# A new issue order and engine choice for all pieces of an attention and mixing kernel

## The chip, the cores and the metric

The kernel runs on one core of a Trainium2 chip. That core has five engines with a queue of their own each: TensorE (PE, with its weight loads shown as PEld), VectorE (DVE), ScalarE (ACT), GpSimd (POOL) and SyncE (SP), which here only issues DMAs. An engine takes its instructions strictly in the order in which the program issues them to it; engines wait for each other through semaphores. The metric is the device time of one execution in microseconds (us). Inputs are drawn at random with a fixed seed and come as 64-bit floats.

## The reference, cut to what matters

```python
# q, k, v: (8, 8, 576, 64); w_theta, w_ch: (512, 512); w_tok_r, w_tok_i: (576, 576)
k_p = k.reshape(B, H, 72, 8, D).mean(axis=3)
v_p = v.reshape(B, H, 72, 8, D).mean(axis=3)
scores = scale * np.matmul(q, k_p.transpose(0, 1, 3, 2))
scores = scores - np.max(scores, axis=-1, keepdims=True)
attn = np.exp(scores)
attn = attn / (np.sum(attn, axis=-1, keepdims=True) + 1e-09)
x = np.matmul(attn, v_p)            # heads joined: (8, 576, 512)
theta = x @ w_theta
zr, zi = x * np.cos(theta), x * np.sin(theta)
y = einsum('ts,bsd->btd', w_tok_r, zr) + einsum('ts,bsd->btd', w_tok_i, zi)
u = x + y
out = u + np.maximum(u @ w_ch, 0.0)
```

## The kernel before, in words

The work is cut into streams, one Python generator for each small unit, and each `yield` in a generator ends a piece. A stream's name is a letter, a batch b (0 to 7) and a number. A written list, SCHEDULE (line 30), names streams word by word: each word issues the next piece of its stream. A last letter v, g or a on a word gives the engine of a piece that has a choice: VectorE, GpSimd or ScalarE. Since an engine takes its instructions in order, the list fixes the order of every queue, SP's DMA queue among them. Waits on data and on buffers are put in by the framework; a buffer with one copy makes its next writer wait for the last reader.

The streams, with the pieces that matter here:

- k, v (`load`) and Q (`queries`): DMAs of batch b; Q then has one VectorE transpose. K b.j and V b.j (`pool`) add up groups of eight rows (line 408, 413) on VectorE or GpSimd; V of batch 0 does so on TensorE (`pool_on_pe`). K b (`keys`) turns the pooled keys into kpT; V b (`vals`) lays out the pooled values (lines 537 to 556).
- h, c (`channel_weights`) and w (`token_weights`): DMA a slice of the 64-bit weights, make 32-bit values of it with five VectorE pieces and one ScalarE piece (`to_f32`, lines 280 to 299), and split h and c into a high and a low part (lines 178, 331). W (`turn_weights`) transposes the token weights on TensorE (line 382) and splits them into WTh and WTl (line 373).
- S b.m (`soften`): scores of 128 rows (TensorE, line 583), maximum, exponential, sum, reciprocal, and the multiply en by the reciprocal (line 644, small remainder line 653), then a transpose. E b (`turn`): sixteen DMAs per group (line 728) finish that transpose, then copies and subtractions give eh, er, ev (lines 742, 749).
- X b.g.c (`attend`): the product with the values (line 775) and its copy to xT.
- T b.m (`rotate`), eleven pieces: xh (a copy, line 176 or 178), xl (a subtraction, line 791), the product pt with w_theta (line 798, twelve matmuls), g on ScalarE (line 802), g on VectorE (line 804), four transposes into the PSUM bank px (line 808), sine, absolute value, cosine (lines 815 to 823), and two products z with px on VectorE (lines 825, 827). px has one bank, pt has one bank (th).
- Z b.c (`take`): zh (copy) and zl (subtraction, line 849). M b.c.hf (`mix`): the token product py (line 862, 27 matmuls), the sum u (line 868), uh (copy), ul (subtraction, line 875). F b.c.hf (`final`): the channel product pf (line 890, 12 matmuls), oT (line 896), the transpose R (line 909, R has one buffer) and four DMAs out (line 915).

A copy shows as line 176 when ScalarE does it and as line 178 on VectorE or GpSimd. Products with high and low parts are sums of three products, which is why each value comes as a pair.

The loop that carries out the list (line 991) is

```python
for word in SCHEDULE.split():
    name, engine = (word[:-1], word[-1]) if word[-1] in "vga" else (word, None)
    now[0] = engine
    next(streams[name])
```

Of the kernel before, what the change touches and what calls it, by code (L numbers as in the profile page):

```python
# [35 lines left out]
S0.2 w0.1v w2.1 w1.1 h3 S0.2g k1.1 w1.1 S0.0a S0.1a S0.4 S0.1 w1.0 S0.2g S0.3 S0.2 S0.1v h3 S0.4 S0.3 w2.0
w1.0 S0.4 X0.0.0 w1.0 S0.3g S0.3v w2.0 h3 w1.0 w2.0 S0.3 h3 w1.0 X0.0.0a S0.4 W0 S0.2a S0.4 Q1.0 w1.0 S0.3a
w1.1 w4.0 h3 X0.0.1 w1.0g W0v Q1.1 h3v S0.2 K1.1g X0.0.1a S0.2v w2.1 S0.4v X0.0.2 S0.4v h3v S0.3 S0.4
X0.0.2a S0.3a S0.4v X0.0.3 W0 w2.0 v1.0 S0.4 K1 X0.0.3a w1.1v K1.2g T0.0a W0 T0.1a w2.0 S0.4v X0.2.0 w3.0
w2.1 T0.0g Q1.1 v1.2 W0a K1a T0.0 X0.2.0a T0.1g w2.1 c0 V1.0v w2.1 K1 X0.2.1 w3.0 T0.0 v1.1 w2.0 w2.1 K1a  # L40
T0.0 X0.2.2 w2.1 X0.2.1v w3.0 T0.0 T0.0 w2.0g W0 w2.1v X0.2.3 X0.2.2a T0.0a w4.0 w3.0 T0.1 T0.0 T0.0 w4.0
V1.1g w3.0 w3.1 T0.0 X0.2.3a w3.0 T0.2a w3.1 W1 T0.1 T0.3v w3.1 T0.2g c0 T0.2 T0.1 W1a V1v w3.1 V1v W1 V1.2g
T0.1 T0.1 T0.1a T0.1 c0 W1 w3.1 T0.2 X0.2.3g k2.2 W1v w4.0 V1 W1 T0.2 T0.2 w4.0 W2 T0.4a T0.1 T0.2 w3.1 T0.1
W2a w4.0 T0.3g T0.3 w3.1v T0.2a W2 T0.2 w3.0g T0.2 W2 T0.3 w4.0 T0.2 W2a T0.3 T0.3 T0.4g T0.4 c0 T0.3 W2 V1v
T0.3a w4.0g V1v T0.3 T0.3 W3 T0.4 c0 T0.3 T0.4 T0.4 W3a c0 T0.4 c0 W3 T0.4 c1 T0.4 W3 c0v W3a Z0.0a W3 c0v
W4 c0v Z0.1a Z0.0v M0.0.0 c1 W4v Z0.1v W4 M0.1.0 c1 W4a M0.0.0 W4 M0.0.0a c1 W4v M0.0.0v W4 c1 W4v c1 W4 c1
M0.0.1 M0.1.0 M0.1.0a c2 c1g M0.1.0v c1v c1g M0.1.1 Z0.2v M0.0.1 c2 Z0.2g M0.0.1a c2 M0.0.1v c2 S1.0 Z0.3a
M0.1.1 M0.1.1v c2 M0.2.0 S1.0 Z0.3g M0.1.1v S1.0 c2 c2 c3 c2v M0.3.0 M0.2.0 c2a M0.2.0v S1.0 M0.2.0v S1.0v
S1.0g c2v c3 S1.1 M0.3.0 c3 M0.3.0a S1.0 S1.1 M0.3.0g M0.2.1 S1.0a c3 S1.1 S1.0 c3 c3 c3 S1.0 S1.1 S1.2
S1.0a M0.2.1 Q2.0 S1.1g S1.1v c3v M0.2.1a M0.3.1 S1.2 S1.0 S1.2 c3v c3g M0.2.1v S1.1 k2.0 M0.3.1 F0.0.0  # L50
S1.1a S1.2 M0.3.1a S1.1 S1.1 M0.3.1v S1.3 S1.2g S1.1v F0.0.1 S1.3 S1.2g K2.0g S1.1 S1.3 F0.0.0 S1.2 F0.0.1
X1.0.0 F0.0.0 F0.1.0 X1.0.0v F0.0.1 F0.0.1 X1.0.1 S1.3 S1.4 F0.1.0 X1.0.1v k2.1 X1.0.2 S1.4 F0.1.1 X1.0.2v
Q2.0 X1.0.3 F0.2.0 S1.2a F0.1.0 Q2.1 X1.0.3a F0.1.1 S1.2 T1.0a S1.2 F0.2.1 S1.2a F0.2.0 S1.3g T1.0v T1.1a
S1.2 S1.3g T1.0 T1.1v S1.4 F0.1.1 K2.1v K2.2g F0.1.1 F0.2.1 S1.3 Q2.1 T1.0 v2.2 F0.3.0 S1.3a v2.0 S1.3 S1.3
F0.3.1 S1.4 S1.3a Q3.0 F0.2.0 S1.4g S1.4v F0.3.0 T1.0 T1.0 S1.3 S1.4 T1.0 F0.2.1 T1.1 V2.0g S1.4v T1.0a
F0.2.1 F0.3.1 S1.4 T1.0 T1.0 T1.0 S1.4 K2 T1.1 S1.4v v2.1 K2a S1.4 T1.1 T1.1 X1.2.0 T1.1 K2 X1.2.0v K2a
T1.1a F0.3.0 X1.2.1 F0.3.1 T1.1 S2.0 T1.1 F0.3.1 X1.2.1a T1.1 V2.1g X1.2.2 S2.0 X1.2.2a X1.2.3 X1.2.3a S2.1
S2.0 V2.2g k3.0 T1.2v V2v T1.2v T1.2 V2v k3.2 T1.3a S2.0 V2 T1.3g X1.2.3v T1.2 T1.4v S2.0g T1.2 T1.2 T1.2
S2.0g S2.1 T1.3 K3.0g T1.2a S2.0 T1.2 T1.2 S2.1 S2.2 T1.2 V2g k3.1 T1.4g V2v T1.3 S2.1 T1.3 T1.3 S2.1g S2.1v
T1.3 S2.2 T1.4 K3.1g T1.3a T1.3 S2.1 S2.2 T1.3 E2.0 T1.3 K3.2g S2.2 S2.3 T1.4 T1.4 S2.2g T1.4 T1.4 K3 T1.4  # L60
S2.2g S2.3 T1.4 S2.3 S2.4 Z1.0v Z1.1a K3v Z1.0v M1.0.0 Z1.1v v3.2 Q3.0 M1.0.1 v3.0 M1.0.0 E2.0a Q3.1 E2.0v
E2.0g S2.2 M1.0.0a S2.3 E2.0g M1.1.0 Z1.2a M1.0.1 S2.3v M1.0.1a S2.3v S2.3 V3.0g S2.4 X2.0.0 M1.1.1 X2.0.0a
Q3.1 S2.4 Z1.2g v3.1 S2.4 Q4.0 M1.1.0 M1.0.0v X2.0.1 M1.1.0v S2.4g Z1.3a M1.0.1v K3 M1.2.0 X2.0.1v K3v
M1.1.0v V3.1g Z1.3v M1.1.1 V3.2v M1.1.1a X2.0.2 k4.0 M1.2.0 S3.0 X2.0.2a M1.1.1v M1.2.0v S2.4v X2.0.3 S2.4
k4.2 M1.2.1 X2.0.3v E2.2 M1.2.0v S3.0 T2.0v S3.0 T2.1v T2.0g K4.0v M1.3.0 T2.1g S3.0 M1.2.1 S3.0g M1.2.1a
S3.1 M1.3.0 S3.0g M1.3.0v M1.2.1g M1.3.1 S3.1 M1.3.0g S3.1 S3.1 k4.1 S3.2 M1.3.1 M1.3.1a F1.0.0 M1.3.1g S3.0
E2.2a E2.2v T2.0 E2.2g E2.2v S3.1g F1.0.0 S3.1v X2.2.0 S3.2 T2.0 K4.1g F1.0.1 X2.2.0a T2.0 S3.2 X2.2.1
F1.0.1 T2.0 T2.0 S3.2 T2.1 v4.0 F1.0.1 F1.0.0 X2.2.1a K4.2v T2.0a F1.0.1 T2.0 T2.0 X2.2.2 T2.0 S3.3 X2.2.2a
v4.2 S3.1 T2.1 X2.2.3 T2.1 S3.2g T2.1 E3.0 X2.2.3a F1.1.0 V3v X2.2.3a T2.1 S3.2g T2.2v T2.3v T2.2g T2.1a
S3.3 T2.2 T2.1 T2.3g T2.1 S3.3 T2.1 F1.1.0 F1.1.1 T2.2 T2.4v F1.1.0 T2.2 T2.2 T2.4v T2.2 T2.3 S3.3 T2.2a  # L70
F1.1.1 T2.2 T2.2 T2.2 F1.2.0 F1.1.1 T2.3 V3v V4.0g V3 F1.1.1 T2.3 T2.3 S3.4 F1.2.0 V3g T2.3 V3g T2.3v T2.4
v4.1 E3.0a Q4.0 T2.3 T2.3 E3.0a Q4.1 E3.0g T2.3 F1.2.1 F1.2.0 T2.4 S3.2 E3.0g T2.4 T2.4 F1.3.0 F1.2.1 T2.4
F1.2.1 T2.4 F1.2.1 F1.3.1 S3.3g T2.4 F1.3.0 Z2.0a S3.3g S3.4 V4.1g X3.0.0 K4 Z2.1a Z2.0v M2.0.0 S3.4 Z2.1g
k5.0 K4v F1.3.1 Q4.1 M2.0.1 M2.0.0 Q5.0 X3.0.0v M2.0.0a V4.2v K5.0v k5.2 M2.1.0 Z2.2a M2.0.1 k5.1 M2.0.0v
F1.3.1 M2.0.1a Z2.2g S3.3 S3.4 K4 M2.0.1v X3.0.1 K4v M2.1.1 M2.1.0 X3.0.1v M2.1.0v K5.1g S3.4v S3.4v F1.3.0
S3.4 F1.3.1 X3.0.2 M2.1.0g M2.1.1 Z2.3a S4.0 X3.0.2v v5.0 K5.2g M2.1.1v X3.0.3 S4.0 M2.2.0 E3.2 Z2.3g
X3.0.3v S4.0 T3.0a T3.1v S4.0 T3.0g M2.2.1 M2.2.0 M2.2.0a M2.2.0v M2.1.1g S4.0g T3.1g M2.3.0 M2.2.1 M2.2.1v
S4.0g M2.2.1g S4.1 M2.3.0 v5.2 M2.3.0v M2.3.1 M2.3.0g S4.1 E3.2v E3.2a S4.1 E3.2v E3.2g S4.0 F2.0.0 M2.3.1
S4.1 S4.2 M2.3.1v S4.1g S4.1v X3.2.0 F2.0.0 S4.2 T3.0 X3.2.0a M2.3.1g S4.1 S4.2 F2.0.0 X3.2.1 S4.2 T3.0
F2.0.1 X3.2.1a T3.0 S4.2g X3.2.2 F2.0.1 S4.2g T3.0 T3.0 F2.0.1 S4.3 X3.2.2v F2.0.1 T3.0v T3.0 T3.0 X3.2.3  # L80
S4.3 T3.1 X3.2.3a E4.0 V4a X3.2.3g T3.2v S4.3 T3.0 T3.2g V4v S4.4 T3.1 T3.3v V5.0g S4.3 V4 F2.1.0 T3.1 T3.1
Q5.0 T3.1 T3.2 T3.3g T3.1a F2.1.0 F2.1.0 T3.1 V4g T3.1 V4g T3.1 F2.1.1 T3.4v T3.2 T3.4g T3.2 T3.2 F2.2.0
F2.1.1 T3.2 v5.1 F2.1.1 T3.2a T3.3 T3.2 T3.2 F2.2.0 Q5.1 S4.2 E4.0a T3.2 S4.3g E4.0a F2.1.1 S4.3v S4.4
F2.2.1 V5.1g T3.3 T3.3 S4.4 T3.3 F2.3.0 S4.3 E4.0g F2.2.1 k6.0 T3.3 S4.4 T3.4 E4.0g Q5.1 T3.3a T3.3 F2.2.0
Q6.0 T3.3 F2.3.1 V5.2g T3.3 F2.2.1 T3.4 F2.3.0 X4.0.0 F2.2.1 F2.3.1 K5 K6.0g T3.4 X4.0.0a T3.4 K5a X4.0.1
# [944 lines left out]
```

## Time and profile before

| | us |
|---|---|
| median of 3 runs (677.22 to 685.16) | 682.79 |
| profiled execution, device time | 678.47 |
| its span, first to last instruction | 676.6 |
| TensorE matmul busy in it | 599.3 |
| VectorE busy | 569.1 |
| ScalarE busy | 315.7 |
| GpSimd busy | 288.4 |

The mean granted TensorE clock was 0.955 of full speed. A busy time is the union of the engine's instructions; groups give the sum or mean of single instructions, which overlap a little at their ends. "Idle before, releaser" is the time in which the engine waited ahead of an instruction of the group, and whose instruction ended the wait. In the rows, `L862 PE MATMUL py<-WTh,zh` reads: line 862, TensorE, output py from WTh and zh.

### The profile page before, as it was taken

What the parts mean: (1) busy time and instruction counts of PE and PEld (TensorE: products, weight loads), DVE (VectorE), ACT (ScalarE), POOL (GpSimd) and SP (SyncE); (2) the same over time, 40 slices, a digit from 0 to 9 for tenths busy, and PEclk for the clock granted to TensorE, in tenths of its full rate; (3) what the DMA queues carried; (4) which work ended last, traced back from release to release, by engine and by line L of the source; (5) the groups of instructions that cost most, each with busy time, mean ns of one, the idle gap of its engine ahead of it and who ended that gap; (6) DMA issues with size and microseconds to landing.
All of it is one profiled execution on the core that took longest, in us unless ns stands there. A gap on an engine that the chain in (4) does not pass through costs nothing.

```text
span 676.6 us, 11101 instructions
## 1 busy us (share of the span) xinstructions
PE 599.3 (89%) x3891; PEld 547.4 (81%) x3891; DVE 569.1 (84%) x1068; ACT 315.7 (47%) x640; POOL 288.4 (43%) x300
## 2 busy tenths in 40 slices
PE   0758967899769899989799999999999999999996
...
DVE  4899998899899999897999999999986788546634
...
PEclk9865977999988999999999999999999999999999
DMA  9998201236725535655275404582443132402204
...
DMA packets 243992, 57.83 MB, mean 85 GB/s; under 512 B 232032, under 2 KB 232544, under 8 KB 243936
## 3 DMA queue, kind: packets, MB, share of 16 engines
...
q14 instruction: 25, 0.20, 0.1%
...
## 4 chain that ended last, share of the span: by engine, by line
DVE 37%; PE 36%; SPq 9%; DMA 6%; issue 5%; ACT 4%; POOL 2%; DVEq 0%; ACTq 0%; POOLq 0%
PE py L862 14%; PE pt L798 8%; PE pf L890 8%; SPq L728 5%; PE pv L775 3%; DVE mx L613 2%; PE s L583 2%; DMA eraw<-G 2%; DVE g L804 2%; DVE kpst L408 2%; SPq L499 2%; DVE sm L634 2%; DVE en L653 1%; DVE G L665 1%; DVE ul L875 1%
## 5 line engine op out<-in xcount | busy, mean ns | idle before, releaser
L862 PE MATMUL py<-WTh,zh 128*128 128x288 f32 x576 | 87.8, 300 | 2.3 <-DVE xT L868 2.0
L862 PE MATMUL py<-WTl,zh 128*128 128x288 f32 x576 | 87.2, 296 | 0.0
L862 PE MATMUL py<-WTh,zl 128*128 128x288 f32 x576 | 85.6, 298 | 0.9 <-DVE xT L868 0.9
L862 PEld LDWEIGHTS py<-WTh,zh 128*128 128x128 f32 x576 | 80.6, 191 | 4.1 <-DVE xT L868 2.4
L862 PEld LDWEIGHTS py<-WTh,zl 128*128 128x128 f32 x576 | 79.6, 190 | 1.2 <-DVE xT L868 1.1
L862 PEld LDWEIGHTS py<-WTl,zh 128*128 128x128 f32 x576 | 80.6, 189 | 0.0
L644 POOL TENSOR_TENSOR en<-e,ri 128x512 f32<-128x512 f32 (+1 forms) x30 | 33.2, 1108 | 70.2 <-DVE ri L641 40.3
L791 POOL TENSOR_TENSOR xl<-xT,xh 128x512 fp32r<-128x512 f32 x27 | 40.6, 1510 | 50.2 <-DVE xh L178 31.4
L798 PE MATMUL pt<-th,xh 128*128 128x512 f32 x160 | 47.8, 421 | 10.1 <-DVE g L804 10.0
L176 ACT CAST uh<-xT 128x288 fp32r<-128x288 f32 x37 | 15.9, 432 | 81.2 <-DVE xT L868 81.1
L583 PE MATMUL s<-kpT,qT 128*128 128x144 f32 (+1 forms) x320 | 48.5, 298 | 5.5 <-DVE e L628 3.5
L849 POOL TENSOR_TENSOR zl<-z,zh 128x1152 fp32r<-128x1152 f32 x12 | 32.2, 2689 | 43.7 <-ACT zh L176 42.1
L868 DVE TENSOR_TENSOR xT<-py,xT 128x288 f32<-128x288 f32 x64 | 28.0, 439 | 27.1 <-PE py L862 27.0
L583 PEld LDWEIGHTS s<-kpT,qT 128*128 128x128 f32 (+1 forms) x320 | 42.9, 185 | 8.5 <-issue 5.2
L890 PE MATMUL pf<-uh,chh 128*128 128x288 f32 x256 | 46.0, 301 | 0.4 <-DVE oT L896 0.4
L798 PE MATMUL pt<-th,xl 128*128 128x512 f32 x160 | 44.2, 399 | 0.4 <-DVE xl L791 0.4
L890 PE MATMUL pf<-ul,chh 128*128 128x288 f32 x256 | 44.3, 295 | 0.0
L890 PE MATMUL pf<-uh,chl 128*128 128x288 f32 x256 | 44.2, 294 | 0.0
L798 PE MATMUL pt<-tl,xh 128*128 128x512 f32 x160 | 44.2, 399 | 0.0
L802 ACT ACTIVATE g<-pt,c_magic 128x512 f32<-128x512 f32 x38 | 26.1, 686 | 38.4 <-PE pt L798 23.8
L798 PEld LDWEIGHTS pt<-th,xh 128*128 128x128 f32 x160 | 28.4, 195 | 18.0 <-DVE g L804 11.4
L890 PEld LDWEIGHTS pf<-uh,chh 128*128 128x128 f32 x256 | 38.1, 189 | 2.6 <-DVE oT L896 1.0
...
## 6 DMA issues: line engine op xcount, KB each, us to landing
...
```

The costliest lines, as they stand in the source:

```text
L176: nc.scalar.copy(out, src)
L583: nc.tensor.matmul(scs[c // 2][:n, 2 * SP * (c % 2) : 2 * SP * (c % 2 + 1)], qT[:, c, t0 : t0 + n], kpT[:, c, :], start=True, stop=True,)
L644: ENG[pick()].tensor_tensor(en[:n, 0:512].rearrange("p (h g) -> p h g", h=8), e[:n, :, 0:GM], ri[:n].unsqueeze(2).broadcast_to([n, 8, GM]) ...
L728: nc.sync.dma_start(blocks(Ex, jj, i), blocks(Gx, i, jj))
L775: nc.tensor.matmul(pv[:, :gn], l, r, start=i == 0, stop=i == len(terms) - 1)
L791: ENG[pick()].tensor_tensor(xl, xT[:, :, o], f32(xh), ALU.subtract)
L798: nc.tensor.matmul(pt, l[:, c, :], r[:, c, :], start=i == 0, stop=i == 11)
L802: nc.scalar.activation(g, pt, AF.Identity, bias=c_magic)
L849: ENG[pick()].tensor_tensor(zl, z[:, :, o], f32(zh), ALU.subtract)
L862: nc.tensor.matmul(py[:, :HALF], l[:, kk, :], r[:, kk, t], start=i == 0, stop=i == 3 * NK - 1)
L868: nc.vector.tensor_tensor(u, py[:, :HALF], u, ALU.add)
L890: nc.tensor.matmul(pv[:, :HALF], l[:, kk, o], uhl[r][:, kk, t], start=i == 0, stop=i == 11)
```

## The change: what it does

The list is written anew: the same 1882 words by stream and count, in another order, and 309 of the 661 words with an engine letter have another letter. Two small edits in the code let pieces of one stream family come in any order: the buffer of pooled rows is made by whichever piece comes first, not by piece 0 or 1 (no instruction is added by it). The pieces themselves stay.

How often each engine has a piece, before and after, for the kinds that change most:

| piece | ACT | DVE | POOL |
|---|---|---|---|
| uh copy of M (64) | 37, 32 | 27, 11 | 0, 21 |
| ul subtraction of M (64) | | 40, 28 | 24, 36 |
| xh copy of T (40) | 17, 19 | 23, 9 | 0, 12 |
| xl subtraction of T (40) | | 13, 14 | 27, 26 |
| zh copy of Z (32) | 25, 22 | 7, 2 | 0, 8 |
| zl subtraction of Z (32) | | 20, 18 | 12, 14 |
| multiply en of S (40) | | 8, 21 | 32, 19 |
| copy to xT of X (64) | 40, 46 | 24, 18 | |
| eh copy of E (12) | 10, 5 | 2, 3 | 0, 4 |
| er subtraction of E (12) | | 2, 4 | 10, 8 |
| ev subtraction of E (12) | | 4, 7 | 8, 5 |
| pooling of K, batch 1 on (14 large) | | 6, 2 | 8, 12 |
| pooling of V, batch 1 on (14 large) | | 1, 5 | 13, 9 |

Order, in the places that the prediction speaks of. The loads begin with w0.0 k0.1 Q0.0 k0.0 k0.2 h0 v0.0 Q0.1 before, and with k0.0 k0.2 k0.1 w0.0 h0 h2 Q0.0 Q0.1 after; w4.0 is issued ahead of v1.0 before, and behind v1.1 after. On VectorE V1's first piece and W1's split stood in the order V1, W1 before; after, V1's first piece is ScalarE's and comes later. Of the ten c0 pieces, all are ahead of the first py before and five after. In batch 7 TensorE's queue reads, with pt and px for the two TensorE pieces of a rotation: pt 7.2, F6.1.0, px 7.2, pt 7.3, F6.1.1, px 7.3 before, and pt 7.2, px 7.2, F6.1.1, pt 7.3, px 7.3 after.

The diff, cut to the first and the last lines of the list and the code:

```diff
 SCHEDULE = """
-w0.0 k0.1 Q0.0 k0.0 w0.0 w0.0 k0.2 w0.0 h0 w0.0 v0.0 w0.0 w0.0 Q0.1 w0.0g Q0.0 K0.0v h2 K0.1v K0.2g h1 K0.0g
-K0.1g h0 K0.0v v0.1 K0.2g h0 K0.1g K0.2v h0 K0 h0 v0.2 V0.0 K0a h3 h0 h0 w0.1 h0 Q0.1 w1.1 K0 K0a S0.0 h0v
...
-T7.1 T7.1 F6.0.1 T7.2 T7.1a T7.3v F6.0.1 T7.1 X7.2.3g T7.1 F6.0.1 T7.1 F6.1.0 T7.4v T7.2 T7.4g T7.2 T7.2
-F6.1.0 T7.2 T7.3 F6.1.0 T7.2a T7.2 T7.2 T7.2 F6.1.1 T7.3 T7.3 T7.3 F6.1.1 T7.3 T7.4 F6.1.1 T7.3a F6.1.1 T7.3
...
+k0.0 K0.0v K0.0g k0.2 K0.2g k0.1 K0.1v K0.1v K0.1g w0.0 w0.0 w0.0 w0.0 K0.0g K0 w0.0 w0.0 h0 h2 h0 h2 h0 h0 h2
+h2 h0 h0 h2 w0.0 K0a K0.2v K0.2g K0 K0a Q0.0 Q0.0 h0 h0 h0a h0g h2 w0.0v Q0.1 Q0.1 S0.0 h1 h1 h2 S0.0 S0.0 S0.0
...
+T7.1 X7.2.3 X7.2.3a T7.3v T7.2a M6.3.1g M6.2.1g F6.0.1 F6.0.1 F6.0.1 T7.1 T7.1a T7.1 T7.1 T7.2g T7.1 T7.2 T7.2
+F6.0.1 T7.2 T7.2 T7.2 T7.2a T7.2 F6.1.1 F6.1.1 T7.2 T7.2 T7.3g T7.3 T7.3 T7.3 T7.3 T7.3 T7.3a T7.3 F6.1.0 F6.1.0
...
+M7.1.0 M7.0.0v M7.1.0 M7.0.1 M7.0.1 M7.0.1v M7.0.1v M7.1.0g M7.1.0g Z7.2g M7.1.1 Z7.2g M7.1.1 M7.2.0 M7.1.1g
+M7.2.0 M7.2.1 M7.2.1 M7.0.0g M7.2.0a M7.2.1a M7.2.1v Z7.3g Z7.3g M7.3.0 M7.3.0 M7.3.0a M7.2.0v M7.3.1 M7.3.1
...
@@ -442,9 +439,9 @@
...
+        if (name, b) not in pooled:
+            pooled[name, b] = [work([P, NC, D], F32, name, f"{name}{b}"), None]
         if j < 2:
-            if (name, b) not in pooled:
-                pooled[name, b] = [work([P, NC, D], F32, name, f"{name}{b}"), None]
             dst = pooled[name, b][0][:, 2 * j : 2 * j + 2, :]
...
     def pool_on_pe(b, name, j, st):
         steps = [dict(start=r == 0, stop=r == POOL - 1) for r in range(POOL)]
-        if j == 0:
+        if (name, b) not in pooled:
             pv = bank([P, 512], "th", f"pvp{b}")
```

More of the change, by code (lines that the diff above doesn't have):

```diff
@@ L36 @@
[L36 to L85, printed above, removed]
```

143 lines of the change are left out of this document (94 added, 49 removed).

## Prediction

> **What bounds the kernel now.** I read the page first (busy shares and the 40 slices), then the table of five stages, then what TensorE waited for, then the groups of instructions that change their engine. The page:
> ```profile
> PE 599.3 (89%) x3891; PEld 547.4 (81%) x3891; DVE 569.1 (84%) x1068; ACT 315.7 (47%) x640; POOL 288.4 (43%) x300
> ...
> PE   0758967899769899989799999999999999999996
> ...
> DVE  4899998899899999897999999999986788546634
> ...
> PEclk9865977999988999999999999999999999999999
> DMA  9998201236725535655275404582443132402204
> ```
> PE is at 9 nearly throughout the second half, and there the order of the other engines can win little. In slices 3 to 19 both PE and DVE are at 7 to 9, and neither alone is the bound. So I cut the span where the stages change: the first scores (23 us), the first mixing product M0.0.0 (108), that of batch 1 (205), that of batch 7 (630). Each row has the length, then busy us and count of PE, PEld, DVE, ACT and POOL, the granted clock and the DMA share:
> ```profile
> 0.00:23.00 23.00, 5.20 (x22) 4.00 (x22) 12.01 (x24) 4.88 (x9) 8.16 (x15) 1.00 0.98 202
> 23.00:108.00 85.00, 60.74 (x256) 42.81 (x257) 82.60 (x159) 49.18 (x150) 40.78 (x35) 0.74 0.55 130
> 108.00:205.00 97.00, 84.47 (x539) 77.00 (x538) 86.23 (x174) 55.84 (x158) 42.32 (x53) 0.94 0.39 81
> 205.00:630.00 425.00, 407.74 (x2770) 382.65 (x2769) 366.23 (x676) 202.19 (x319) 193.68 (x195) 1.00 0.42 77
> 630.00:677.00 47.00, 41.14 (x311) 40.90 (x309) 22.04 (x39) 3.65 (x7) 3.48 (x2) 0.97 0.20 35
> ```
> Up to 23 us the DMA engines set the pace (share 0.98). From 23 to 108 it is VectorE, with 82.6 of 85 us busy, while PE idles 24.3 us. From 108 to 205 PE idles 12.5 us and DVE 10.8: they take turns. From 205 on PE idles 17.3 of 425 us, and that is all that any order can win there. What PE waited for, in total us, times, and the longest:
> ```profile
> PE wt L382 <- DVE WTl L373: 10.3, 2, 5.9
> PE pt L798 <- DVE g L804: 10.0, 9, 3.5
> PE pe L677 <- POOL spare L644: 4.0, 1, 4.0
> PE s L583 <- DVE e L628: 3.5, 2, 3.0
> ```
> DVE releases most of it. The first and third row lie wholly in the stage from 23 to 108.
>
> **The change part by part.** The instructions stay: no shape, DMA or product changes. What moves is place in each queue and, for part of the copies and subtractions, the engine. The groups that change most (busy us, mean ns), then the copies with min/median/max ns:
> ```profile
> L791 POOL TENSOR_TENSOR xl<-xT,xh 128x512 fp32r<-128x512 f32 x27 | 40.6, 1510 | 50.2 <-DVE xh L178 31.4 <-ACT xh L176 18.0 <-PE pf L890 0.6
> L644 POOL TENSOR_TENSOR en<-e,ri 128x512 f32<-128x512 f32 (+1 forms) x30 | 33.2, 1108 | 70.2 <-DVE ri L641 40.3 <-DVE G L668 16.0 <-ACT g L802 7.0
> L849 POOL TENSOR_TENSOR zl<-z,zh 128x1152 fp32r<-128x1152 f32 x12 | 32.2, 2689 | 43.7 <-ACT zh L176 42.1 <-DVE zh L178 1.6
> L875 DVE TENSOR_TENSOR ul<-xT,uh 128x288 fp32r<-128x288 f32 x40 | 27.6, 690 | 5.5 <-ACT uh L176 5.1
> L875 POOL TENSOR_TENSOR ul<-xT,uh 128x288 fp32r<-128x288 f32 x24 | 19.5, 814 | 46.5 <-ACT uh L176 39.4 <-DVE uh L178 7.0
> L178 DVE CAST xh<-xT 128x512 fp32r<-128x512 f32 x23 | 16.7, 740 | 1.0 <-ACT xT L176 0.8
> L178 DVE CAST uh<-xT 128x288 fp32r<-128x288 f32 x27 | 14.4, 532 | 0.5
> L644 DVE TENSOR_TENSOR en<-e,ri 128x512 f32<-128x512 f32 (+1 forms) x8 | 6.4, 804 | 0.0
> ```
> ```profile
> L178 DVE CAST uh<-xT x27: 258/310/2523, 125.7 to 648.9; 128x288 fp32r<-128x288 f32 x27
> L178 DVE CAST xh<-xT x23: 377/420/3873, 81.3 to 612.2; 128x512 fp32r<-128x512 f32 x23
> L178 DVE CAST zh<-z x7: 1295/1341/1353, 120.2 to 637.0; 128x1152 fp32r<-128x1152 f32 x7
> L178 POOL COPY xT<-xT x5: 387/398/860, 83.0 to 610.1; 128x256 f32<-128x256 f32 x5
> ```
> The counts are those of the table of the change. DVE loses 16 uh x 0.53 = 8.5 us, 12 ul x 0.69 = 8.3, 14 xh x 0.74 = 10.4 and 5 zh x 1.34 = 6.7, and gains 13 multiplies by the reciprocal x 0.80 = 10.4: 23.5 us less of 569. The other moves go both ways, and I take them as nothing. POOL gains 12 ul x 0.81 = 9.8 us and casts that it has not done before: 21 uh, 12 xh, 8 zh. Its nearest row is the copy of 256 elements in 398 ns, 1.55 ns an element, which gives 0.45, 0.79 and 1.79 us, or 33.2 us in all; the two-input row (2689 ns for 1152, 2.33 an element) bounds them above at 50. I take the copy's price, since a cast also reads one input. POOL loses 13 multiplies x 1.11 = 14.4. Net about +29 us, at most +45, on 288. ACT gains some 7 us on 316 and stays far from full.
>
> VectorE and GpSimd slow each other. Both cast rows have a mean far above the median: 27 x (0.532 - 0.310) = 6.0 us and 23 x (0.740 - 0.420) = 7.4 us were lost, with single casts of 2.5 and 3.9 us. So taking 30 of those 50 casts off DVE removes victims as well, and more POOL work hits those left.
> [...]
>
> *Start to 108 us.* Loads: k of batch 0 is now issued first, h2 moves ahead of the queries and v0.0 behind them; ahead of the first scores stand the same number of bytes (v0.0 and h2 are half a megabyte each), so these start near 23 us again. DVE has h2's steps to do meanwhile. Ahead of M0.0.0, 15 steps come to DVE (four xl, three multiplies, one pooling of K1, small ones) and 25 leave its queue (five of c0, four of V1, theta and W casts to ACT); at some 0.8 us for what comes and 0.7 for what goes that is 12 against 17.5, 5 us less. POOL is relieved too: 4 xl x 1.51 and the long multiply below alone are 10.5 us. The rows show that multiply on POOL, a copy of V1 on DVE, and PE's wait that ends with the split of W1:
> ```profile
> 37.36 4.46 POOL L644 TENSOR_TENSOR spare<-spare,ri 128x512 f32<-128x512 f32 x1 [4.49 <-DVE ri L641]
> ...
> 83.39 3.06 DVE L178 CAST Vh<-vp 64x256 fp32r<-64x256 f32 x2
> ...
> 89.32 0.47 PE L382 MATMUL wt<-ident,wsrc_a 128*128 128x128 f32 x1 [5.89 <-DVE WTl L373]
> ```
> The multiply takes 4.46 us on POOL (0.80 on DVE), and PE's 4.0 us wait is for it. Vh stands ahead of WTl on DVE; in the new order V1's first step goes to ACT and W1's WTl follows its copy with nothing of V1 between. I take another 3 us for this: **-8 us** for the stage. Best case the two waits of 14.3 us, worst +3 if w4.0, now issued behind v1.0 and v1.1, comes late.
>
> *108 to 205 us.* The c steps put off above come here, V1's steps go to POOL and ACT, and DVE comes out about even. PE and DVE alternate as before: **-2 us**, between -6 and +4.
>
> *205 to 630 us.* DVE is at 366 of 425 us and gets most of its relief of 23 us here. PE's 17.3 us of idle time go mostly to DVE releases; I take a third of it, **-5 us**, because the rotations get tighter covers (first rival). Bounds -12 and +9.
>
> *Tail.* Same order of products, the last out transfers as before: 0. The new POOL chain of batch 7 (zh and zl of chunks 1 to 3, 4.5 us each at the prices above) fits under the two products py of each chunk, whose row stands with the first rival.
>
> Sum -15 us. The profiled execution took 678.5 us (span 676.6, with 1.9 around it), the median of the runs 682.8, 4.3 more. 678.5 - 15 = 663.5; I add 1.5 for a part of that offset and say **665 us**.
>
> **The rivals.** *Slower: the transposes px wait for the rotation before them.* px has one bank. The transposes of rotation m+1 can start only when the second product with px of rotation m is done. One such chain, with the cover now:
> ```profile
> 611.32 1.08 PE L798 MATMUL pt<-th,xl 128*128 128x512 f32 x4
> ...
> 612.44 0.69 ACT L802 ACTIVATE g<-pt,c_magic 128x512 f32<-128x512 f32 x1 [1.71 <-PE pt L798]
> ...
> 613.16 0.69 DVE L804 SCALAR_TENSOR_TENSOR g<-g,pt 128x512 f32<-128x512 f32 x1 [0.57 <-ACT g L802]
> ...
> 615.21 0.72 ACT L823 ACTIVATE g<-g,c_cos 128x512 f32<-128x512 f32 x1
> ...
> 616.79 0.48 DVE L909 STREAM_TRANSPOSE R<-oT 128x288 f32<-128x288 f32 x1 [2.31 <-DMA out_dram<-R]
> ...
> 617.77 0.67 DVE L827 TENSOR_TENSOR z<-px,g 128x512 f32<-128x512 f32 x1
> ...
> 618.62 0.61 PE L808 MATMUL px<-ident,xT 128*128 128x128 f32 x4
> ```
> ```profile
> 340.99 1.59 PE pf L890 x12
> ...
> 344.60 2.76 PE pt L798 x12
> ...
> 434.67 3.56 PE py L862 x27
> ```
> From pt's end (612.4) to z's end (618.44) are 6.0 us; without the R that waited, 615.93 + 0.67 gives 4.2. Before, PE had between them 1.59 + 0.61 + 2.76 + 1.59 = 6.55 us of work; in the new order pt and px stand back to back, and 0.61 + 1.59 + 2.76 = 4.96 us are left. Eight rotations (three of batch 2, one each of 5 and 6, three of 7) have about 5 in this way. At 4.2 nothing happens; at 6.0 each stalls 1.1, 9 us; at 7, also where the cover is still 6.5, some 22 us. With 8 won at the start that is +14: 692 us. It decides from a chain of about 6.7 us on. Against it: in the new order of batch 7, j and k follow without an R ahead of them.
>
> *No change.* POOL's extra 29 to 45 us take back on DVE what its casts gave up, and the waits merely change names: 679 us, 672 to 686. For it: the 13.4 us lost by two groups alone, while POOL had 288 us. Against: most victims leave.
>
> *Faster still: TensorE's clock.* From 23 to 108 us it was granted 0.74, and PE's 60.7 busy us would be 45 at 1.00. If the new order closes the waits of 4.0 and 5.89 us and the clock stays full, PE stops standing beside DVE in that stage: another 7 to 15 us, 650 us. [...]
>
> **How the numbers follow.** Forecast 0.50 (652 to 675), faster still 0.12, no change 0.20, slower 0.18. The range takes the stages' bounds without the outer tenth at each end: 643 to 692. About 1% is what a measurement of this kernel can tell from no change. Faster by over 1%: the forecast, faster still, less a little of the forecast's upper end, 0.61; within: 0.20; slower 0.19.
>
> **What would show it.** Right: M0.0.0 near 98 to 101 us instead of 108; DVE some 25 us less busy in all, POOL 25 to 45 more; no PE wait for POOL's multiply and under 5 us for WTl; the uh cast on POOL near 0.45 us and zh near 1.8. The rival: px L808 waiting for z L827 with more than 5 us. Wrong: casts on POOL of 2.3 ns an element or more with zh on the chain that ended last, M0.0.0 later than 108, or PE idle above 20 us between batch 1's and batch 7's first product.

## The result and the profile after

The changed kernel takes 655.4 us (median of 4 runs, 653.8 to 657.7), the kernel before, beside it, 684.0 (677.2 to 685.9): a ratio of 0.960, 95% interval 0.953 to 0.968. Forecast were 665 us in a range of 643 to 692. The profiled execution has a span of 653.4 us where that of before had 676.6: 23.2 us less. TensorE was idle 17.3 us less of these and busy 5.9 us less (599.3 to 593.4) with the same 3891 matmuls, at a mean granted clock of 0.968 instead of 0.955.

The page of the changed kernel: busy times with instruction counts, then slices, then the chain that ended last.

```profile
PE 593.4 (91%) x3891; PEld 544.5 (83%) x3891; DVE 498.2 (76%) x987; ACT 315.4 (48%) x675; POOL 303.8 (47%) x342
...
PE   0567988999779989999999999999999999999996
...
DVE  3879898898687798868898787788877898556424
...
PEclk9985888999989999999999999999999999999999
...
PE 56%; DVE 21%; ACT 9%; DMA 4%; SPq 4%; issue 3%; POOL 2%; DVEq 0%; ACTq 0%; POOLq 0%
```

VectorE is 70.9 us less busy (569.1 to 498.2), GpSimd only 15.4 us more, ScalarE the same. TensorE is at 9 without a break from the 16th slice to the last but one, before from the 21st. The same five stages as in the prediction, each cut where its first instruction now starts (length, then busy us and count of PE, PEld, DVE, ACT, POOL, granted clock, DMA share):

```profile
0.00:23.00 23.00, 2.18 (x8) 1.49 (x9) 10.92 (x26) 5.43 (x10) 5.93 (x14) 1.00 0.95 185
23.00:100.80 77.80, 60.34 (x270) 43.94 (x269) 68.56 (x142) 51.34 (x157) 23.50 (x22) 0.82 0.57 141
100.80:193.20 92.40, 82.32 (x540) 74.75 (x538) 76.76 (x163) 62.88 (x182) 40.88 (x60) 0.96 0.45 92
193.20:606.30 413.10, 407.02 (x2765) 382.97 (x2766) 324.44 (x625) 194.06 (x324) 217.17 (x235) 0.99 0.42 78
606.30:653.00 46.70, 41.59 (x314) 41.36 (x313) 17.51 (x33) 1.73 (x4) 16.34 (x13) 1.00 0.21 37
```

By the first products: M0.0.0 starts at 100.8 us (107.8 before), M1.0.0 at 193.2 (205.3), M7.0.0 at 606.3 (629.7). So the start won 7.0 us (forecast 8), the stage to M1.0.0 5.1 (forecast 2), the steady stage 11.3 (forecast 5), the tail nothing (forecast 0). In the steady stage TensorE now idles 413.1 - 407.0 = 6.1 us, where it idled 17.3. What is left of its waits (total us, times, longest):

```profile
PE pk L469 <- POOL kp L410: 13.3, 2, 12.1
PE pkr L477 <- POOL kpr L410: 8.1, 1, 8.1
PE wt L379 <- DVE WTl L370: 5.6, 2, 3.2
PE s L580 <- DVE e L625: 3.2, 2, 2.6
...
PE pe L674 <- DVE spare L641: 2.0, 1, 2.0
...
PE px L805 <- DVE z L824: 1.2, 2, 0.8
```

(Line numbers are three lower than in the kernel before.) The first two rows are nearly all ahead of the first scores, where TensorE waits for pooled keys; it did so for 16.9 us before. The nine waits for g ahead of pt, 10.0 us, are down to two of 0.6 us together, and px waits 1.2 us in all.

### The profile page after: what moved, and what is told of

Its sections match the earlier page's. It is cut to its first block, busy times and chain, and to the rows that moved or that the text cites. A ratio compares the mean times of both kernels' runs of the same rounds, so it can differ in the third digit from the quotient of the medians.

```text
span 653.4 us, 11040 instructions
## 1 busy us (share of the span) xinstructions
PE 593.4 (91%) x3891; PEld 544.5 (83%) x3891; DVE 498.2 (76%) x987; ACT 315.4 (48%) x675; POOL 303.8 (47%) x342
## 4 chain that ended last, share of the span: by engine, by line
PE 56%; DVE 21%; ACT 9%; DMA 4%; SPq 4%; issue 3%; POOL 2%; DVEq 0%; ACTq 0%; POOLq 0%
PE py L859 27%; PE pf L887 11%; PE pt L795 9%; PE pv L772 5%; PE s L580 3%; SPq L725 2%; DVE mx L610 2%; DMA WTh_st<-in_moe_w_theta_dram 2%; DVE g L801 1%; DVE z L824 1%; PE px L805 1%; ACT g L820 1%; DVE e L625 1%; DVE oT L893 1%; DVE eraw L746 1%
## 5 line engine op out<-in xcount | busy, mean ns | idle before, releaser
L872 POOL TENSOR_TENSOR ul<-xT,uh 128x288 fp32r<-128x288 f32 x36 | 31.9, 893 | 45.0 <-ACT uh L173 36.3
L795 PE MATMUL pt<-th,xh 128*128 128x512 f32 x160 | 47.1, 417 | 3.6 <-ACT xh L173 1.2
L846 POOL TENSOR_TENSOR zl<-z,zh 128x1152 fp32r<-128x1152 f32 x14 | 38.4, 2744 | 23.7 <-ACT zh L173 23.1
L173 ACT CAST uh<-xT 128x288 fp32r<-128x288 f32 x32 | 13.6, 430 | 72.0 <-DVE xT L865 72.0
L629 ACT ACTIVATE e<-e 128x576 f32<-128x576 f32 (+1 forms) x30 | 20.6, 686 | 50.0 <-DVE e L625 49.8
L788 POOL TENSOR_TENSOR xl<-xT,xh 128x512 fp32r<-128x512 f32 x26 | 34.2, 1319 | 22.3 <-ACT xh L173 11.7
L795 PEld LDWEIGHTS pt<-th,xl 128*128 128x128 f32 x160 | 31.2, 196 | 10.6 <-POOL xl L788 3.6
```

Of the source, the lines that this page charges most:

```text
L173: nc.scalar.copy(out, src)
L629: nc.scalar.activation(e[:n], e[:n], AF.Exp, scale=scale)
L788: ENG[pick()].tensor_tensor(xl, xT[:, :, o], f32(xh), ALU.subtract)
L795: nc.tensor.matmul(pt, l[:, c, :], r[:, c, :], start=i == 0, stop=i == 11)
L846: ENG[pick()].tensor_tensor(zl, z[:, :, o], f32(zh), ALU.subtract)
L872: ENG[pick()].tensor_tensor(ul[:, c, t], u, f32(uh[:, c, t]), ALU.subtract)
```

## The experiments

My theory was the prediction's: pieces leave VectorE, which is then less busy and less held up by GpSimd, and TensorE stops waiting for it. The rivals: the order does it whatever the engines, or each only works with the other. Ratios are to the kernel before, run on the same chip, with 95% intervals. The kernel before took 684.0 us beside the changed kernel (median of 4) and 678.3 to 679.8 beside the others (medians of 13), so the changed kernel's ratio can be compared with another's only to about 0.7 points (a point is 0.01 of a ratio). No kernel here leaves out any work.

| kernel | ratio | interval | span us | DVE busy |
|---|---|---|---|---|
| changed | 0.960 | 0.953 to 0.968 | 653.4 | 498.2 |
| order_new | 1.141 | 1.135 to 1.146 | 770.8 | 551.7 |
| letters_new | 1.025 | 1.020 to 1.031 | 694.3 | 523.9 |
| mix_letters | 1.043 | 1.039 to 1.047 | 705.4 | 512.2 |
| att_letters | 1.087 | 1.081 to 1.093 | 736.7 | 535.5 |
| start_new | 0.995 | 0.992 to 0.998 | 674.0 | 558.4 |
| start_old | 0.973 | 0.967 to 0.978 | 657.5 | 509.0 |
| casts_dve | 0.997 | 0.994 to 1.000 | 674.9 | 522.5 |
| casts_place | 0.981 | 0.977 to 0.986 | 664.0 | 526.9 |
| casts_early | 0.973 | 0.969 to 0.977 | 659.1 | 512.3 |
| casts_act | 1.004 | 1.001 to 1.007 | 680.6 | 500.7 |
| casts_more | 0.978 | 0.973 to 0.983 | 664.0 | 492.9 |
| s0_en | 0.962 | 0.959 to 0.966 | 650.5 | 497.5 |

### The order alone, the engines alone

order_new, against the changed kernel (one line of many):

```diff
-M7.1.0 M7.0.0v M7.1.0 M7.0.1 M7.0.1 M7.0.1v M7.0.1v M7.1.0g M7.1.0g Z7.2g M7.1.1 Z7.2g M7.1.1 M7.2.0 M7.1.1g
+M7.1.0 M7.0.0v M7.1.0 M7.0.1 M7.0.1 M7.0.1a M7.0.1v M7.1.0a M7.1.0v Z7.2v M7.1.1 Z7.2v M7.1.1 M7.2.0 M7.1.1a
```

> The new order with every old engine letter. All work stays. If the gain of about 28 us comes from the order (pieces of one stream issued together, other neighbours for VectorE's and GpSimd's instructions), VectorE's busy time falls here too, from 569 to about 510 us, and the time is 20 to 28 us shorter than before (ratio 0.96 to 0.97). If it comes from the engine choice (casts off VectorE, fewer pairs in which it and GpSimd slow each other), VectorE stays at 555 to 570 and the time is within 10 us of before (0.985 to 1.00); since the new order was written for other queues, it could then also be slower. My theory is a share for both: VectorE near 545, -10 us, 0.985.

letters_new, against the kernel before:

```diff
-K0.1g h0 K0.0v v0.1 K0.2g h0 K0.1g K0.2v h0 K0 h0 v0.2 V0.0 K0a h3 h0 h0 w0.1 h0 Q0.1 w1.1 K0 K0a S0.0 h0v
+K0.1v h0 K0.0g v0.1 K0.2v h0 K0.1g K0.2g h0 K0 h0 v0.2 V0.0 K0a h3 h0 h0 w0.1 h0 Q0.1 w1.1 K0 K0a S0.0 h0a
```

> The old order with every new engine letter. All work stays. If the engine choice carries the gain, VectorE falls to about 500 us busy (569 less 21 for the pieces moved, less some 50 of the time lost beside GpSimd) and the time is 18 to 28 us shorter than before (0.96 to 0.975). If the order carries it, VectorE is at 535 to 550 (the pieces alone), and the time is within 8 us of before (0.99 to 1.01). My theory: VectorE near 520, -12 us, 0.98.

No number that I had named comes near this (only for the order was a slower kernel named as possible): each alone makes the kernel slower, the order by 14%, the engines by 2.5%, and together they make it 4% faster. It is not VectorE's load, which fell in both, as the first lines of the two pages show:

```profile
PE 624.2 (81%) x3891; PEld 565.5 (73%) x3891; DVE 551.7 (72%) x1068; ACT 310.2 (40%) x636; POOL 286.7 (37%) x300
```
```profile
PE 606.5 (87%) x3891; PEld 553.0 (80%) x3891; DVE 523.9 (75%) x987; ACT 320.7 (46%) x679; POOL 302.1 (44%) x342
```

17.4 us less in the one, 45.2 in the other, 70.9 in both together: the busy times nearly add up, the run times don't at all. What a queue out of step does is seen in order_new's trace between 412 and 430 us. GpSimd's queue (start, us, line, instruction, idle time before and its releaser):

```profile
412.81 2.72 POOL L846 TENSOR_TENSOR zl<-z,zh 128x1152 fp32r<-128x1152 f32 x1
415.48 2.11 POOL L405 TENSOR_TENSOR vpst<-vpst 128x512 f32<-128x512 f32 x2
...
423.08 2.09 POOL L405 TENSOR_TENSOR kpst<-kpst 128x512 f32<-128x512 f32 x2 [3.34 <-DMA kpst<-in_k_dram]
...
425.66 1.26 POOL L641 TENSOR_TENSOR en<-e,ri 128x512 f32<-128x512 f32 x1
426.88 3.09 POOL L746 TENSOR_TENSOR eraw<-eraw,eh 128x1280 fp32r<-128x1280 f32 x1
```

ScalarE's, SP's and TensorE's queues in the same stretch:

```profile
415.18 1.27 ACT L173 CAST eh<-eraw 128x1280 fp32r<-128x1280 f32 x1 [9.70 <-DMA eraw<-G]
```
```profile
418.25 8.72 SPq L422 DMA_DIRECT2D kpst<-in_k_dram  x4
```
```profile
430.02 0.63 PE L772 MATMUL pv<-eraw,Vh 128*128 128x320 f32 x1 [5.54 <-POOL eraw L746]
```

A long subtraction stands on GpSimd ahead of the pooling of v; the loads of the next k are issued when that pooling is done; GpSimd then waits 3.3 us for these loads, with en and eraw queued behind; TensorE waits 5.5 us for eraw. The input eh of the subtraction that gives eraw was ready at 416.4 us, and the subtraction started at 426.9: what made it late is what stood in front of it. From M1.0.0 to M7.0.0 TensorE idles 68 us in all (501.0 long, 433.0 busy); only this stretch was followed.

### Which letters the new order needs

mix_letters is the new order with the new engines of T, Z, M and X only, att_letters with those of the other streams only.

```diff
-k0.0 K0.0v K0.0g k0.2 K0.2g k0.1 K0.1v K0.1v K0.1g w0.0 w0.0 w0.0 w0.0 K0.0g K0 w0.0 w0.0 h0 h2 h0 h2 h0 h0 h2
+k0.0 K0.0v K0.0g k0.2 K0.2g k0.1 K0.1v K0.1g K0.1g w0.0 w0.0 w0.0 w0.0 K0.0v K0 w0.0 w0.0 h0 h2 h0 h2 h0 h0 h2
```

> The new order, the new engines for the pieces of T, Z, M and X (xh, xl, zh, zl, uh, ul, the copies to xT: 184 of the 309 letters) and the old ones for the rest (S, E, K, V, weights). The new order with all the old letters took 776 us. Theory: there GpSimd's long subtractions zl and xl (2.7 and 1.4 us) stand ahead of the pooling of k and v, which releases the DMAs of the softmax groups on SP's queue; then most of the 120 us between that kernel and the changed one return here: 665 to 690 us (0.98 to 1.015). Rival: the multiplies en, the pooling and the E pieces on the wrong engine cause it, then 730 us or more here.

```diff
-T0.0a T0.0v w2.0 T0.1a w2.1 w1.1 S0.4 S0.4a S0.4 S0.4a T0.0 X0.2.1 w2.0 T0.0 w1.1 X0.2.1a Q1.1 Q1.1 w1.1g w3.0
+T0.0a T0.0g w2.0 T0.1a w2.1 w1.1 S0.4 S0.4a S0.4 S0.4a T0.0 X0.2.1 w2.0 T0.0 w1.1 X0.2.1v Q1.1 Q1.1 w1.1g w3.0
```

> The complement: the new order, the new engines for S, E, K, V and the weights (125 letters), the old ones for T, Z, M and X. By the theory above it keeps most of the loss, 730 us or more (1.075); by the rival 660 to 690 us. If each half is near 715 to 720, the losses are of no one family: any piece on an engine whose queue was not laid out for it holds up what stands behind.

1.043 and 1.087. Against the changed kernel's 0.960 the old letters of the softmax side cost 8 points, those of the mixing side 13, both together 18. Neither the theory (0.98 to 1.015 for the first) nor its rival holds: the loss is of no one family. Both halves leave VectorE with 34 to 57 us less work than before and are slower than before.

### The 41 copies

The plainest engine choice of the change is 41 copies (21 uh, 12 xh, 8 zh) that GpSimd now does. casts_dve puts them back on VectorE, casts_act on ScalarE; the order and every other letter stay.

```diff
-M7.1.0 M7.0.0v M7.1.0 M7.0.1 M7.0.1 M7.0.1v M7.0.1v M7.1.0g M7.1.0g Z7.2g M7.1.1 Z7.2g M7.1.1 M7.2.0 M7.1.1g
+M7.1.0 M7.0.0v M7.1.0 M7.0.1 M7.0.1 M7.0.1v M7.0.1v M7.1.0v M7.1.0g Z7.2v M7.1.1 Z7.2g M7.1.1 M7.2.0 M7.1.1v
```

> The changed kernel with its 41 copies on GpSimd (21 uh, 12 xh, 8 zh) back on VectorE, nothing else moved. By the medians of the copies on VectorE (0.31, 0.42, 1.34 us) that is 22 us more work there: 498 to 520 us busy. If these copies were also the main victims of GpSimd's work, VectorE rises by more, to 530 or above, and the time is about 668 us (ratio to before 0.98). If the loss left for another reason (which instructions stand beside each other), VectorE is at 520 or less and the time within 5 us of the changed kernel's 655 (0.96 to 0.967). A third outcome, that their place in the new order is what counts: over 680 us, as when all the letters are put back.

```diff
-M7.1.0 M7.0.0v M7.1.0 M7.0.1 M7.0.1 M7.0.1v M7.0.1v M7.1.0g M7.1.0g Z7.2g M7.1.1 Z7.2g M7.1.1 M7.2.0 M7.1.1g
+M7.1.0 M7.0.0v M7.1.0 M7.0.1 M7.0.1 M7.0.1v M7.0.1v M7.1.0a M7.1.0g Z7.2a M7.1.1 Z7.2g M7.1.1 M7.2.0 M7.1.1a
```

> The changed kernel with the 41 copies on ScalarE (0.43 us for a uh, some 0.6 for an xh, 1.2 for a zh: about 24 us more on 315). If it only counts that they leave VectorE, the time is that of the changed kernel (0.955 to 0.967). If it counts which queue they stand in (ScalarE's holds sines that wait for VectorE, exponentials that wait for the maximum), part of casts_dve's loss is here too: 0.97 to 0.99.

The 41 copies alone undo the gain: 0.997 on VectorE, 1.004 on ScalarE. The pages' first lines:

```profile
PE 597.1 (88%) x3891; PEld 546.4 (81%) x3891; DVE 522.5 (77%) x1028; ACT 315.3 (47%) x675; POOL 277.7 (41%) x301
```
```profile
PE 599.2 (88%) x3891; PEld 547.9 (80%) x3891; DVE 500.7 (74%) x987; ACT 338.1 (50%) x716; POOL 274.4 (40%) x301
```

casts_act is the sharper of the two. VectorE is as free there as in the changed kernel (500.7 against 498.2) and ScalarE is busy half the time, and yet nothing of the gain is left. So a freer VectorE is not enough by itself. In casts_dve VectorE has 24.3 us more (22 by the copies' medians), but M4.0.0 starts only 0.9 us later than in the changed kernel (406.6 against 405.7); the rest of the 21.5 us of span comes behind. VectorE's queue in batch 7 of casts_dve, and TensorE's wait:

```profile
641.38 0.46 DVE L865 TENSOR_TENSOR xT<-py,xT 128x288 f32<-128x288 f32 x1 [1.38 <-PE py L859]
644.98 0.46 DVE L865 TENSOR_TENSOR xT<-py,xT 128x288 f32<-128x288 f32 x1 [3.14 <-PE py L859]
645.94 0.46 DVE L872 TENSOR_TENSOR ul<-xT,uh 128x288 fp32r<-128x288 f32 x1 [0.50 <-ACT uh L173]
646.31 1.34 DVE L175 CAST zh<-z 128x1152 fp32r<-128x1152 f32 x1
```
```profile
647.71 1.46 PE L859 MATMUL py<-WTh,zh 128*128 128x288 f32 x9 [2.77 <-DVE zh L175]
```

z is complete since 616.4 us, but zh stands behind a sum u that waits 3.1 us for TensorE's product, and TensorE's next product needs zh: VectorE idles, then TensorE. On GpSimd the same copy stands behind an earlier uh (of M7.1.1) and not behind the two sums u of chunk 2: it starts 16.8 us after M7.0.0 there (623.14), and 26.7 us after it here. On ScalarE it stands behind the copy uh, which waits for that u:

```profile
652.01 0.43 ACT L173 CAST uh<-xT 128x288 fp32r<-128x288 f32 x1 [3.17 <-DVE xT L865]
652.35 1.15 ACT L173 CAST zh<-z 128x1152 fp32r<-128x1152 f32 x1
```
```profile
653.55 2.53 PE L859 MATMUL py<-WTh,zh 128*128 128x288 f32 x9 [2.07 <-ACT zh L173]
```

If this is the cause, the copies can stay on VectorE and cost less when they are only listed earlier. casts_place does that with four copies of batch 7 (X7.2.3's last piece goes ahead with the xh that needs it):

```diff
-F6.0.1 T7.2 T7.2 T7.2 T7.2a T7.2 F6.1.1 F6.1.1 T7.2 T7.2 T7.3g T7.3 T7.3 T7.3 T7.3 T7.3 T7.3a T7.3 F6.1.0 F6.1.0
-T7.3 T7.3 F6.1.0 F6.1.1 F6.1.1 X7.2.3g T7.4v T7.4g T7.4 T7.4 T7.4 T7.4 T7.4 T7.4 F6.2.1 F6.2.1 T7.4 Z7.0a Z7.0g
+F6.0.1 T7.2 T7.2 T7.2 T7.2a T7.2 F6.1.1 F6.1.1 T7.2 T7.2 T7.3g T7.3 T7.3 X7.2.3g T7.4v T7.3 T7.3 T7.3 T7.3a T7.3
+F6.1.0 F6.1.0 T7.3 T7.3 F6.1.0 F6.1.1 F6.1.1 T7.4g T7.4 T7.4 T7.4 T7.4 T7.4 T7.4 F6.2.1 F6.2.1 T7.4 Z7.0a Z7.0g
...
-F6.2.0 F6.2.0 F6.2.0 F6.2.1 F6.2.1 F6.3.0 F6.3.0 F6.3.1 F6.3.1 F6.3.1 F6.3.0 F6.3.1 M7.0.0 M7.0.0 Z7.1v Z7.1g
-M7.1.0 M7.0.0v M7.1.0 M7.0.1 M7.0.1 M7.0.1v M7.0.1v M7.1.0v M7.1.0g Z7.2v M7.1.1 Z7.2g M7.1.1 M7.2.0 M7.1.1v
-M7.2.0 M7.2.1 M7.2.1 M7.0.0g M7.2.0a M7.2.1a M7.2.1v Z7.3v Z7.3g M7.3.0 M7.3.0 M7.3.0a M7.2.0v M7.3.1 M7.3.1
+F6.2.0 F6.2.0 F6.2.0 F6.2.1 F6.2.1 F6.3.0 F6.3.0 F6.3.1 F6.3.1 F6.3.1 F6.3.0 F6.3.1 Z7.1v M7.0.0 M7.0.0 Z7.1g
+M7.1.0 M7.0.0v M7.1.0 M7.0.1 Z7.2v M7.0.1 M7.0.1v M7.0.1v M7.1.0v M7.1.0g M7.1.1 Z7.2g M7.1.1 M7.2.0 M7.1.1v
+Z7.3v M7.2.0 M7.2.1 M7.2.1 M7.0.0g M7.2.0a M7.2.1a M7.2.1v Z7.3g M7.3.0 M7.3.0 M7.3.0a M7.2.0v M7.3.1 M7.3.1
```

> As casts_dve (all 41 copies on VectorE), but in batch 7 four of these copies stand some places earlier in the list: zh of chunk 1 ahead of the first product py, zh of chunks 2 and 3 ahead of the sum u that VectorE waits for, xh of the last rotation ahead of the preceding rotation's waits. The work on VectorE is the same, 522 us. If the copies cost time because they stand behind VectorE's waits for TensorE, the four stalls of TensorE there (3.3, 1.8 and 2.8 us in the trace, and the half clock after them) go, and the time falls from 678 to 667 to 672 us (ratio 0.98 to 0.988). If VectorE's load is what costs, it stays at 676 to 680 (0.997).

0.981 (666.0 us, against 678.2 for casts_dve), with VectorE busier, not less busy (526.9 us against 522.5). Its stage from M7.0.0 on:

```profile
614.80:663.00 48.20, 42.58 (x316) 41.65 (x314) 23.14 (x38) 1.73 (x4) 12.34 (x8) 1.00 0.21 37
```

From M7.0.0 to the end of the span are 48.9 us (615.1 to 664.0), in casts_dve 55.3 (619.6 to 674.9), in the changed kernel 47.1 (606.3 to 653.4). Moving four copies by a few places won back 10.9 of the 21.5 us that the 41 letters had cost. For this half of the loss the place decides, not the load; the other 10.6 us were not taken apart.

casts_early puts the copies of batches 0 to 4 on VectorE, 20 of the 41:

```diff
-Z4.2g Z4.2g X5.0.1 X5.0.1a M4.1.0 M4.1.0 M4.1.0g X5.0.2 X5.0.2v M4.0.1g M4.0.1g M4.1.1 M4.1.1 M4.1.1g V6.2g Q6.1
+Z4.2v Z4.2g X5.0.1 X5.0.1a M4.1.0 M4.1.0 M4.1.0v X5.0.2 X5.0.2v M4.0.1v M4.0.1g M4.1.1 M4.1.1 M4.1.1v V6.2g Q6.1
```

> The changed kernel with only the copies of batches 0 to 4 back on VectorE (20 of the 41: 12 uh, 5 xh, 3 zh), some 10 us more work there. With all 41 back M4.0.0 started within 1 us of the changed kernel's, and the 22 us were lost behind it. If the place alone decides, the time is within 3 us of the changed kernel's (0.958 to 0.966). If each copy costs its share of the load, half the loss is seen: 665 us or more (0.978).

0.973, between the two numbers expected, so it decides little: 5.7 us of span are lost, all of it by the start of M5.0.0 (481.4 us against 475.7). It does show that these copies are not all harmless, as I had read from M4.0.0 of casts_dve.

casts_more gives GpSimd the 22 copies that VectorE had kept as well:

```diff
-M7.1.0 M7.0.0v M7.1.0 M7.0.1 M7.0.1 M7.0.1v M7.0.1v M7.1.0g M7.1.0g Z7.2g M7.1.1 Z7.2g M7.1.1 M7.2.0 M7.1.1g
+M7.1.0 M7.0.0g M7.1.0 M7.0.1 M7.0.1 M7.0.1g M7.0.1v M7.1.0g M7.1.0g Z7.2g M7.1.1 Z7.2g M7.1.1 M7.2.0 M7.1.1g
```

> The changed kernel with the 22 copies of these kinds that VectorE has kept (11 uh, 9 xh, 2 zh) on GpSimd as well: 10 us less there, 12.5 us more on GpSimd's 304. If VectorE's load still costs, it is 2 to 6 us faster than the changed kernel (0.951 to 0.957). If the place decides, these copies now stand behind GpSimd's long subtractions and it is slower by 5 us or more (over 0.967).

0.978, slower than the changed kernel by 1.8 points, although VectorE falls to 492.9 us. Moving more of the same the same way doesn't help either.

### The start

start_new has the new list up to M0.0.0's first piece, then the rest in the old order with the old letters; start_old the reverse. The words around the seam:

```diff
-W4 c0v Z0.1a Z0.0v M0.0.0 c1 W4v Z0.1v W4 M0.1.0 c1 W4a M0.0.0 W4 M0.0.0a c1 W4v M0.0.0v W4 c1 W4v c1 W4 c1
+c0 c0 W4 Z0.0a Z0.0v V1v V1v V1 V1v V1v c0 c0 c1 c0v c0v c0v Z0.1a M0.0.0 c1 W4v Z0.1v W4 M0.1.0 c1 W4a M0.0.0
```

> The new list (order and engines) up to the first piece of M0.0.0, the first mixing product, and from there the old list and engines. The start was 7.0 of the 23 us in the two profiles. If the gains of the stages add up, M0.0.0 starts near 101 us after the span's start and the time is 7 us shorter than before (0.99). If the early start only moves the wait (VectorE still full behind it), the time is within 3 us of before. If the start's order also serves what follows, -12 us or more (0.982).

```diff
-c0 c0 W4 Z0.0a Z0.0v M0.0.0 c0 c0 c0v Z0.1a Z0.1v c0a V1a V1g c0v M0.0.0 M0.0.0a M0.0.0g W4a W4 W4a W4 W4a W4
+T0.4 W3a c0 T0.4 c0 W3 T0.4 c1 T0.4 W3 c0v W3a Z0.0a W3 c0v W4 c0v Z0.1a Z0.0v M0.0.0 Z0.1v M0.0.0 M0.0.0a
```

> The old list and engines up to the first piece of M0.0.0, and from there the new ones. If the gains of the stages add up, M0.0.0 starts near 108 us and the time is 16 to 21 us shorter than before (0.97 to 0.976), with VectorE behind 205 us as free as in the changed kernel. If the rest needs the new start (pieces of c0 and V1 that it leaves for later), less than 12 us (above 0.982).

0.995 and 0.973. The start alone is worth half a per cent, the rest alone 2.7. In start_new M0.0.0 is at 100.8 us as in the changed kernel, but the next stage gives it all back:

```profile
100.60:205.10 104.50, 85.85 (x541) 76.88 (x539) 92.25 (x189) 57.99 (x163) 42.62 (x53) 0.94 0.38 80
205.10:626.80 421.70, 407.25 (x2764) 383.12 (x2765) 364.06 (x675) 202.40 (x319) 193.92 (x195) 1.00 0.41 77
```

M1.0.0 starts at 205.3 us, exactly as before. The pieces of c0 and V1 that the new start leaves out fall on a VectorE that is busy 92 of 104 us. The 7 us were borrowed. With the new list behind it the new start is worth 4.1 us of span (653.4 in the changed kernel against 657.5 in start_old): there VectorE is busy 76.8 of the next 92.4 us, and has room for these pieces.

s0_en puts batch 0's multiplies (three, and two remainders) back on GpSimd:

```diff
-h1 h1 h1 h2 S0.1 S0.1 h1 S0.1 h1 v0.0 S0.1 S0.0 S0.0 h1 v0.1 h3 V0.0 h3 V0.1 v0.2 S0.0v S0.0v V0a V0.2 V0 S0.2
+h1 h1 h1 h2 S0.1 S0.1 h1 S0.1 h1 v0.0 S0.1 S0.0 S0.0 h1 v0.1 h3 V0.0 h3 V0.1 v0.2 S0.0g S0.0g V0a V0.2 V0 S0.2
```

> The changed kernel with batch 0's five multiplies by the reciprocal that moved to VectorE (S0.0, S0.1, S0.3 and two remainders) back on GpSimd. In the profile before, one of them took 4.46 us there and TensorE waited 4.0 us for it. If the start's gain of 7 us has this term, M0.0.0 starts 3 to 4 us later (104 instead of 101 us after the span's start) and the time is 2 to 4 us longer than the changed kernel's (ratio to before 0.963 to 0.966); if the multiply is hidden there, no difference (0.96).

0.962, no difference that can be measured, and M0.0.0 is at 99.8 us. The multiply that took 4.46 us in the kernel before takes 1.05 here, on the same engine:

```profile
39.16 1.05 POOL L641 TENSOR_TENSOR spare<-spare,ri 128x512 f32<-128x512 f32 x1 [1.21 <-DVE ri L638]
```

## Why the prediction was right, and where it was not

The direction was right, and so was the start's size (7.0 against 8); the sum of -15 us fell short of the measured 23.2 by 8 us of span. Taken by its steps:

- **"DVE 23.5 us less of 569"**: 70.9 less. What I counted only as an aside, instructions held up beside GpSimd, fell by more than the work did. An estimate from the fourteen traces takes the 20th percentile of each kind of instruction as what it costs by itself. By this, VectorE's instructions cost 533 us before and 505 after, so the 28 us of work that left were priced a little low (23.5). The time that they took beyond it, whatever held them up, fell from 91 to 36 us (sums of single instructions). One row of it in each kernel, the small remainder of the multiply en, on VectorE both times:

```profile
L653 DVE TENSOR_TENSOR en<-e,ri 128x32 f32<-128x32 f32 (+1 forms) x42 | 18.6, 482 | 0.0
```
```profile
L650 DVE TENSOR_TENSOR en<-e,ri 128x32 f32<-128x32 f32 (+1 forms) x46 | 8.2, 218 | 0.2
```

   I had expected the relief from fewer victims. But this group has four instructions more, GpSimd has 15 us more work, and the time is halved: what fell is the number of unlucky meetings. Over all kinds, the instructions that took more than 1.5 times their own cost fell from 101 to 38. In the traces of these two kernels all of them ran beside a GpSimd instruction. VectorE's instructions that ran beside none took 1.01 times their own cost, estimated from these two alone (559 in the kernel before, 527 in the changed one), the others 1.34 times before (509) and 1.12 after (460). GpSimd's took 1.12 and 1.09 times theirs beside a VectorE instruction and 1.00 beside none. The order and the engines each gave a part: the time beyond is 66 us in order_new and 66 in letters_new. By itself it is not enough for a faster kernel, as casts_act shows: 38 us there, and no gain.
- **"POOL +29, at most +45"**: +15.4. The copies were priced by the copy of 256 elements at 1.55 ns an element; that fits uh (0.43 us, forecast 0.45) but not the longer ones, so that the 41 copies cost 25.5 us and not 33.2. By the same estimate the work that came to GpSimd is 24 us, and the time beyond it fell from 31 to 23. The 7 us more that I gave ScalarE did not come (315.7 to 315.4). The copies (minimum, median and maximum ns):

```profile
L175 POOL CAST uh<-xT x21: 414/427/1819, 121.9 to 622.0; 128x288 fp32r<-128x288 f32 x21
...
L175 POOL CAST xh<-xT x12: 602/611/632, 155.5 to 590.0; 128x512 fp32r<-128x512 f32 x12
...
L175 POOL CAST zh<-z x8: 1140/1146/1335, 338.2 to 623.1; 128x1152 fp32r<-128x1152 f32 x8
```

- **"-8 us" for the start**: -7.0, but the terms were off. VectorE's busy time up to M0.0.0 fell by 15.1 us (94.6 to 79.5, the first two stages), where I had counted 5. Moving the multiply of 4.46 us is worth nothing (s0_en). GpSimd is not slow at it (1.05 us in s0_en); what made it long in the kernel before was not taken apart. TensorE's wait for WTl went from 10.3 to 5.6 us, near the "under 5" that I had named. And the 7 us are no gain by themselves (start_new).
- **"I take a third of it, -5 us"** in the steady stage: the mis-sized term. TensorE's 17.3 us of idle time fell by 11.2, two thirds.
- **The step that failed** is the one under all of this: that a piece's engine may be costed by its busy time, the order beside it, and that VectorE's relief is what TensorE gets. By that sum letters_new, casts_act and casts_more had to be fast and casts_place no faster than casts_dve. In each of these the busy time points one way and the measurement the other. That the sum had the right direction for the whole change was in part luck, since it has the same direction for letters_new, which is 2.5% slower. The place that a piece gets in an engine's queue can outweigh its duration, and so an engine choice has no price apart from the order.
- **The slower rival** (px) did not come: px waits 1.2 us in total. **No change** fell with its mechanism, since VectorE's hold-ups shrank (91 to 36 us by the estimate above) though GpSimd had more to do. **Faster still, TensorE's clock**: the granted clock from 23 us to M0.0.0 did rise from 0.74 to 0.82. The waits of 4.0 and 5.9 us only shrank, to 2.0 and 3.2, and the clock still stood at 0.50 from 45.5 to 69.4 us (before, from 39.2 to 69.9); that it stays full where such waits close was not shown. By the first two rows of both tables, the same 278 matmuls up to M0.0.0 took 65.9 us of busy time before (5.20 + 60.74) and 62.5 after (2.18 + 60.34). So up to M0.0.0 TensorE was busy 3.4 us less and idle 3.6 us less. The rival's mechanism came in part, with at most 3.4 us where I had named 7 to 15, and the forecast had no term for it.

Open: order_new's 68 us of idle time were followed along one chain only. That the meetings of VectorE and GpSimd became fewer is estimated above from the traces; what this is worth in run time, apart from the places, was not separated, and by casts_act it may be little. How much of each loss is waiting and how much the lower clock behind a wait was not separated either.
